# A dilated convolution with gates on one core: the first block's transposed remainder copied by VectorE alone, the last two gates in tiles of their own, the last stores dealt 5, 5, 2

## The chip, the cores and the metric

The kernel runs on one core of a Trainium2 chip. The metric is the device time of one execution in microseconds. Before the change, three runs took 313.39, 313.51 and 313.54 us; the median is 313.51 us.

The engines are named as in the profile: PE is TensorE (PEld its weight loads), ACT is ScalarE, DVE is VectorE, POOL is GpSimd and SP is SyncE, which only issues transfers here.

## What is computed

```python
B, T, D, K = (2, 16000, 144, 15)          # x: (B, T, D), w: (K, D, 2 * D), w_o: (D, D), all bf16
dil = 2
pad = (K - 1) * dil
xp = jnp.pad(x, ((0, 0), (pad, 0), (0, 0)))
h = sum(jnp.einsum('btc,cd->btd', xp[:, pad - i * dil:pad - i * dil + T, :], w[i]) for i in range(K))
z = jnp.tanh(h[..., :D]) * _sigmoid(h[..., D:])
return z @ w_o
```

It is a causal convolution of 15 taps with dilation 2 from 144 to 288 channels, a gate, and a projection back to 144 channels. (The loop over the taps is written as one sum here.)

## The kernel before

**Work.** The positions are split into eleven blocks: five pairs of full blocks (even and odd positions) and a short last one. Each block gives two units of work, the last block one, so there are 21 units, 0 to 20. A unit computes twelve columns of outputs for 128 rows. Of the 144 input channels the first 128 go through PE as they are; the other 16, the *remainder*, are gathered for eight taps at a time into one further matmul with the weights `Wr`.

**Sums.** The taps are combined with a fast convolution scheme. From the loaded tile `xn` VectorE forms, for each block, sums and differences S, D and E and from these S2, S4, S42, D2, D4, D42, E2 and E4 (line 316, as most of VectorE's work). From the weights it and PE with ScalarE form the matching tap sums `G`, `Gm`, `H`, `HH`, `GD` once at the start (lines 554 and 572; PE sums weights by matmuls with an identity). A unit has four streams, S, D, F and G. For a stream PE does the steps VV, V2a, V2b, for S and D also AV, and then A00, A01, A10, A11; ScalarE copies between the PSUM pairs in between (cVV at line 677, cV at line 683, eAV at line 695) and reads out S and D (ev, line 761); VectorE combines them into `y` (av, U, y1, y0F, y1F, y0G, y1G). Then come tanh and sigmoid (th and sg, lines 744 and 746), their product z (zm), a transposing transfer, the projection (OP0 and OP1) and its copy (os, line 882).

**Remainder of the first block.** For most blocks the transposed remainder R comes by transfers. For the first block `sums_front` makes it at lines 413 to 434: PE transposes sixteen 128x128 pieces into the two banks of a PSUM pair (trR, line 420); ScalarE copies the first bank to R and VectorE the second (cpR, line 427, 128x1024 bf16 each); PE then writes zeros over both banks (zR, line 432), which frees the pair. This is done twice, for units 0 and 1. The F and G parts of `Wr` are loaded by fifteen small transfers from GpSimd's queue (wrl, line 540); VectorE forms the S and D parts from them (wr).

**The end.** The last unit's outputs go out in twelve columns. Columns 8 to 11 (stream F) and 0 to 3 (stream G) are gated, transposed on PE (tr, line 844), copied out by VectorE (cp, line 855) and projected (OPe, line 491); columns 4 to 7 take a transfer (z4T) and one projection. ScalarE copies the results (ose, lines 830 and 852), and each column is stored by a transfer of its own (line 914). The gates of G are for columns 0 and 1 together, then 2, then 3. Each of these gates takes the only buffer of `th8` and of `sg8` with `new(0)`, so it waits for the users of the one before it. For columns 2 and 3, y1G is two sums of 128x288.

**What sets the order.** The table `ORDER` lists for each engine, for SP's transfers (DMA) and for the PSUM pairs (banks) in which order the steps are emitted; `place` goes through these lists and uses costs and latencies (the arguments of `add`) only to interleave them. Each engine and each queue works its list from front to back.

Of the kernel before, what the change touches and what calls it, by code (L numbers as in the profile page):

```python
# [26 lines left out]
def t_dve(n, psum=False):  # L27
# [7 lines left out]
   -1/wsum#10 wsum#6 wsum#12 wsum#4 wsum#16 wsum#8 wsum#2 wsum wsum#14 0/VVF V2bF V2aF VVG -1/trR 0/V2aG V2bG A01F A11F -1/zR 0/A10F A00F A00G A11Fr  # L35
   A01G A10Fr A00Fr A10G A01Fr A11G A00Gr A01Gr 1/AVS 0/VVS A11Gr A10Gr AVS V2aS V2bS -1/trR#1 0/A00S A01S A11S A00Sr A01Sr -1/zR#1 0/A10S VVD A10Sr
   A11Sr AVD V2aD V2bD 1/VVS 0/A01D A00D A01Dr A00Dr 1/V2aS V2bS 0/A11D A10D A11Dr A10Dr 1/A00S A01S A10S AVD VVD A11S V2aD V2bD VVF A10D A11D A00D
   A01D V2bF V2aF VVG 2/AVS 1/A00F A01F V2bG V2aG A10F A11F A11G 2/VVS 1/A10G A00G 2/V2bS V2aS 1/A01G 2/AVD A01S A00S VVD A10S A11S V2bD V2aD 1/OP0
   2/VVF A11D A10D A00D A01D V2aF V2bF 3/AVD 2/VVG A01F A00F A10F V2bG V2aG A11F 1/OP1 2/A00G 3/VVS 2/A01G A11G A10G 3/V2aS V2bS AVS VVD A11S A10S V2bD
   V2aD A01S A00S VVF A01D A00D A11D A10D V2bF V2aF 2/OP0 3/VVG A11F A10F 4/AVS 3/V2bG V2aG A01F A00F 2/OP1 3/A00G 4/VVS 3/A01G A10G A11G 4/V2bS V2aS  # L40
   AVD VVD A10S A11S V2aD V2bD A00S A01S VVF A01D A00D A11D A10D V2bF V2aF 5/AVD 4/VVG A11F A01F A00F A10F V2bG V2aG 3/OP1 OP0 4/A00G 5/VVS 4/A01G
   5/AVS V2bS V2aS 4/A10G A11G 5/VVD A11S A10S V2bD V2aD A00S A01S VVF A00D A01D A10D A11D V2bF V2aF 4/OP0 5/VVG A01F A00F 6/AVS 5/A10F A11F V2aG V2bG
   4/OP1 6/VVS 5/A11G A10G A00G A01G 6/V2aS V2bS AVD VVD A10S A11S V2bD V2aD A01S A00S VVF A11D A10D A01D A00D V2aF V2bF 7/AVD 6/VVG A01F A11F A00F
   A10F V2aG V2bG 5/OP1 OP0 6/A11G 7/VVS 6/A10G 7/AVS V2aS V2bS 6/A00G 7/VVD 6/A01G 7/A00S V2aD V2bD A01S A10S A11S A11D VVF A10D A01D A00D V2bF V2aF
   6/OP0 7/VVG A10F A11F 8/AVS 7/A01F A00F V2bG V2aG 6/OP1 8/VVS 7/A00G A01G 8/AVD V2aS V2bS 7/A10G 8/VVD 7/A11G 8/A01S A00S V2bD V2aD A10S A11S VVF
   A01D A00D A11D A10D V2bF V2aF 9/AVD 8/VVG A01F A11F A10F A00F V2bG V2aG 7/OP1 OP0 8/A11G A10G 9/VVS 8/A01G A00G 9/V2aS V2bS AVS VVD A11S A10S V2aD
   V2bD A00S A01S VVF A00D A01D A10D A11D V2bF V2aF 8/OP0 9/VVG A01F A11F A00F A10F 10/AVS 9/V2bG V2aG 8/OP1 10/VVS 9/A01G A00G 10/AVD V2aS V2bS 9/A10G
   10/VVD 9/A11G 10/A01S V2aD V2bD A00S A10S A11S A11D VVF A10D A01D A00D V2aF V2bF 11/AVD 10/VVG A10F A00F V2aG A11F 9/OP1 10/A01F V2bG 9/OP0 11/VVS
   10/A10G A11G A01G A00G 11/V2aS V2bS AVS VVD A11S A10S V2bD V2aD A00S A01S VVF A10D A11D V2bF V2aF A01D A00D 10/OP0 11/A10F VVG A01F 12/AVS 11/A11F
   A00F V2aG V2bG 10/OP1 12/VVS 11/A00G A01G 12/AVD V2bS V2aS 11/A11G 12/VVD 11/A10G 12/A01S V2bD V2aD A00S A10S A11S A00D VVF A01D A11D A10D V2aF V2bF  # L50
# [194 lines left out]
def kernel(  # L245
# [157 lines left out]
    def sums_front(want):  # L403
# [7 lines left out]
        for r in range(2):  # L411
# [11 lines left out]
            for h, (eng, c) in enumerate((("ACT", t_act(8 * P)), ("DVE", t_dve(8 * P)))):  # L423
                def cp(h=h, pr=pr, R=R):
                    src = banks[pr.slot][:, h, 0:512].bitcast(BF16)
                    dst = R.tile[:, 2 * h:2 * h + 2].rearrange("p s k n -> p (s k n)")
                    K_(nc.vector.tensor_copy(out=dst, in_=src) if h else nc.scalar.copy(out=dst, in_=src))  # L427
# [292 lines left out]
    def unit(ui, bi, r, base):  # L720
# [57 lines left out]
        for k, j in (("F", 2), ("G", 0)):  # L778
            op = ALU.add if k == "F" else ALU.subtract
            for b2, pair in enumerate(conv(bi, r, k, base, AT, av)):  # L780
# [7 lines left out]
                for c, n in ((0, 1), (1, 1)) if last and k == "G" and b2 else ((0, 2),):  # L788
# [3 lines left out]
                    if last and k == "G":  # L792
                        gate(c0 + c, n, t0 + .8)
# [203 lines left out]
```

## Time and profile before

| | |
|---|---|
| runs (3) | 313.39 to 313.54 us, median 313.51 |
| profiled execution | 313.12 us |
| its span, first to last instruction | 311.3 us |
| mean granted TensorE clock | 0.993 |
| busy: PE, VectorE, ScalarE, GpSimd | 297.5, 276.5, 269.0, 27.0 us |
| first matmul of unit 0 | 14.46 us |
| last projection's start | 305.29 us |
| last two stores' issue on ScalarE | from 306.18 us, 2.35 us |

Rows of the timeline give start, duration, engine, line, operation, output and inputs; in brackets stands how long the engine was idle before, and what ended that. A row with `x8` merges eight instructions. Matmul ends are modelled, so a PE gap is best read from the starts of matmuls.

### The profile page before, as it was taken

To read this page: it belongs to the slowest core of one execution; us is meant where nothing else is said; L and a number is where in the kernel's file an instruction comes from. 1 tells how busy PE (TensorE), PEld (TensorE's weight loads), DVE (VectorE), ACT (ScalarE), POOL (GpSimd) and SP (SyncE) were. 2 spreads that over 40 slices of the span, in tenths; PEclk is the share of its full clock that TensorE was granted. 3 is DMA by queue.
4 is the path that set the end of the run, shared out by engine and by line. 5 is a ranking of instruction groups with operands and counts; after the bars stand their busy time and mean duration, and the time that the engine had idled before them with its cause. 6 is when DMAs were issued, how large, how long until landed. Compare 5 with 4: busy or idle time off the path is not lost.

```text
span 311.3 us, 6703 instructions
## 1 busy us (share of the span) xinstructions
PE 297.5 (96%) x2604; PEld 276.5 (89%) x2604; DVE 276.5 (89%) x393; ACT 269.0 (86%) x449; POOL 27.0 (9%) x63
## 2 busy tenths in 40 slices
PE   8998899999999999999999999999999999999981
PEld 3797789999999999999999999999999999999881
DVE  4878999999999999899999999989996998899861
ACT  1658789998989989999998999989888999989982
POOL 9830500000000000000000000000000000000013
PEclk9999999999999999999999999999999999999997
DMA  7995569597799866986796698455886647254344
GB/s 199 107 127 118 150 67 174 140 115 153 126 162 282 215 159 104 142 199 155 189 210 98 118 181 182 138 127 162 146 187 80 123 141 231 73 128 114 59 170 131
DMA packets 153110, 45.78 MB, mean 147 GB/s; under 512 B 137061, under 2 KB 151701, under 8 KB 153078
## 3 DMA queue, kind: packets, MB, share of 16 engines
q1 hardware_dynamic: 151610, 44.59, 69.6%
q0 software_dynamic: 1216, 0.70, 1.1%
q8 instruction: 20, 0.33, 0.5%
q14 instruction: 12, 0.10, 0.1%
q10 hardware_dynamic: 252, 0.06, 0.1%
HBM read 13.31 MB, written 11.84 MB: 81 GB/s over the span
## 4 chain that ended last, share of the span: by engine, by line
PE 80%; ACT 13%; DVE 3%; issue 3%; DVEq 0%; ACTq 0%
PE acc L491 77%; ACT m L761 4%; ACT acc L683 3%; PE acc L527 2%; ACT acc L677 1%; ACT sg L746 1%; ACT th L744 1%; ACT R L427 1%; DVE D L316 1%; DVE S L316 1%; PE acc L420 1%; DVE y L316 1%; ACT os L882 0%; ACT av L695 0%; ACT osl L852 0%
## 5 line engine op out<-in xcount | busy, mean ns | idle before, releaser
L491 PEld LDWEIGHTS <-E 128*128 128x128 bf16 x882 | 112.2, 145 | 7.9 <-issue 4.0
L491 PE MATMUL acc<-w_all,E 128*128 128x288 bf16 x630 | 101.2, 286 | 1.0 <-ACT acc L683 0.3
L491 PE MATMUL acc<-Wr,R 128*128 128x288 bf16 x336 | 94.9, 286 | 0.0
L316 DVE TENSOR_TENSOR y<-U,acc 128x576 bf16<-128x576 bf16 (+1 forms) x81 | 59.4, 744 | 9.9 <-PE acc L491 6.5
L683 ACT ACTIVATE acc<-acc 128x576 f32<-128x576 f32 x84 | 54.1, 645 | 7.2 <-PE acc L491 4.9
L761 ACT ACTIVATE m<-acc 128x576 bf16<-128x576 f32 x84 | 52.8, 651 | 4.3 <-PE acc L491 2.9
L491 PEld LDWEIGHTS <-S 128*128 128x128 bf16 x378 | 48.2, 137 | 5.2 <-issue 2.4
L491 PEld LDWEIGHTS <-D 128*128 128x128 bf16 x378 | 48.8, 137 | 4.0 <-issue 1.1
L677 ACT ACTIVATE acc<-acc 128x288 f32<-128x288 f32 x84 | 33.7, 401 | 8.0 <-PE acc L491 6.4
L746 ACT ACTIVATE sg<-y 128x576 bf16<-128x576 bf16 (+3 forms) x45 | 38.9, 872 | 0.5 <-DVE y L316 0.4
L744 ACT ACTIVATE th<-y 128x576 bf16<-128x576 bf16 (+3 forms) x45 | 38.9, 871 | 0.2
L882 ACT CAST os<-acc 128x864 bf16<-128x864 f32 x40 | 34.6, 880 | 2.0 <-DVE y L316 0.9
L316 DVE TENSOR_TENSOR m<-m,av 128x1152 bf16<-128x1152 bf16 x42 | 30.5, 753 | 6.5 <-ACT m L761 6.3
L491 PE MATMUL acc<-wo_ab,zT 128*128 128x144 bf16 x480 | 35.2, 226 | 0.1
L491 PEld LDWEIGHTS <-zT 128*128 128x128 bf16 x480 | 32.2, 98 | 1.5 <-issue 0.3
L491 PEld LDWEIGHTS <-R 128*128 128x128 bf16 x336 | 32.8, 98 | 0.2
L491 PE MATMUL acc<-G,S 128*128 128x288 bf16 x147 | 30.3, 286 | 0.4 <-ACT acc L683 0.2
L491 PE MATMUL acc<-Gm,D 128*128 128x288 bf16 x147 | 29.7, 285 | 0.3
L695 ACT ACTIVATE av<-acc 128x576 bf16<-128x576 f32 x42 | 27.2, 648 | 3.0 <-PE acc L491 2.4
L491 PE MATMUL acc<-H,E 128*128 128x288 bf16 x168 | 28.1, 286 | 1.1 <-ACT acc L677 1.1
L316 DVE TENSOR_TENSOR E<-E 128x1792 bf16<-128x1792 bf16 (+1 forms) x22 | 28.1, 1286 | 0.0
L316 DVE TENSOR_TENSOR z<-th,sg 128x576 bf16<-128x576 bf16 (+3 forms) x45 | 25.5, 573 | 2.1 <-ACT sg L746 1.4
(75 smaller groups left out, 330.0 us busy)
## 6 DMA issues: line engine op xcount, KB each, us to landing
R<-q SPq DMA_DIRECT2D x19, 512.0 KB
out_dram<-os SPq DMA_DIRECT2D x8, 864.0 KB
q<-T SPq DMA_DIRECT2D x10, 256.0 KB
out_dram<-os SPq DMA_DIRECT2D x2, 519.8 KB
xt<-in_x_dram SPq DMA_DIRECT2D x6, 156.0 KB
w_all<-in_w_dram SPq DMA_DIRECT2D x3, 288.0 KB
out_dram<-os SPq DMA_DIRECT2D x2, 337.5 KB
zT<-z SPq DMA_TRANSPOSE x20
```

The source lines that it names most:

```text
L316: return K_(nc.vector.tensor_tensor(out=out_, in0=a, in1=b, op=op))
L420: K_(nc.tensor.transpose(to, ap(st.tile, c, [1, P]), ident[:, 0, :]))
L427: K_(nc.vector.tensor_copy(out=dst, in_=src) if h else nc.scalar.copy(out=dst, in_=src))
L491: K_(nc.tensor.matmul(bank, lhsT=l(), rhs=r, start=start and q == 0, stop=end and q == len(jobs) - 1, skip_group_check=True))
L527: K_(nc.tensor.matmul(banks[i % 4][:, (i // 4) % 2, :], lhsT=wz[:, 0:P], rhs=wz[:], start=True, stop=True))
L677: add("ACT", t_act(D2), lambda: K_(nc.scalar.activation(out=banks[X.slot][:, 1, 0:D2], in_=banks[X.slot][:, 0, 0:D2], func=ACT.Copy, scale ...
L683: s = add("ACT", t_act(2 * D2), lambda: K_(nc.scalar.activation(out=banks[Y.slot][:, :, 0:D2], in_=banks[X.slot][:, :, 0:D2], func=ACT.Cop ...
L695: add("ACT", t_act(2 * D2), lambda: K_(nc.scalar.activation(out=av.tile[:, SPLIT.index(k)], in_=banks[W.slot][:, :, 0:D2], func=ACT.Copy, ...
L744: add("ACT", t_act(n * D, False), lambda: K_(nc.scalar.activation(out=a_, in_=y_[0], func=ACT.Tanh)), r=[*need, y], w=[th], want=t0, name= ...
L746: add("ACT", t_act(n * D, False), lambda: K_(nc.scalar.activation(out=b_, in_=y_[1], func=ACT.Sigmoid)), r=[*need, y], w=[sg], want=t0 + . ...
L761: add("ACT", t_act(2 * D2), lambda pair=pair, i=i, b2=b2: K_(nc.scalar.activation(out=m.tile[:, i, 2 * b2:2 * b2 + 2, :], in_=banks[pair.s ...
L882: K_(nc.scalar.copy(out=dst, in_=banks[pr.slot][:, :, 0:3 * D].rearrange("p h (q d) -> p h q d", d=D)))
```

## The change

Three steps are edited, four costs that only guide the order are set anew, and the whole `ORDER` table is written in another order.

```diff
-            for h, (eng, c) in enumerate((("ACT", t_act(8 * P)), ("DVE", t_dve(8 * P)))):
-                def cp(h=h, pr=pr, R=R):
-                    src = banks[pr.slot][:, h, 0:512].bitcast(BF16)
-                    dst = R.tile[:, 2 * h:2 * h + 2].rearrange("p s k n -> p (s k n)")
-                    K_(nc.vector.tensor_copy(out=dst, in_=src) if h else nc.scalar.copy(out=dst, in_=src))
-                add(eng, c, cp, r=[pr.part[h]], w=[R], pairs=[pr], want=want + 2 + 8 * r, name="cpR")
+            def cp(pr=pr, R=R):
+                src = banks[pr.slot][:, :, 0:512].bitcast(BF16)
+                dst = R.tile[:].rearrange("p (h s) k n -> p h (s k n)", h=2)
+                K_(nc.vector.tensor_copy(out=dst, in_=src))
+
+            add("DVE", 0.07 + 16 * P / 1700, cp, r=[*pr.part], w=[R], pairs=[pr], want=want + 2 + 8 * r, name="cpR")
...
-            add("POOL", 0.55, lambda k=k, j=j0 + j, c=c: K_(nc.gpsimd.dma_start(out=Wr[c:c + CR, KI[k], :], in_=w[j, P:D, :])), w=[gWr[k]], want=-27, lat=6.0, name="wrl")
+            add("POOL", 0.55, lambda k=k, j=j0 + j, c=c: K_(nc.gpsimd.dma_start(out=Wr[c:c + CR, KI[k], :], in_=w[j, P:D, :])), w=[gWr[k]], want=-27, lat=5.0, name="wrl")
...
-            th, sg = (v[4 if n == 4 else 8].new(0) for v in (th_b, sg_b))
+            own = last and n < 4
+            th, sg = (Gen(v[8].gens[0]) if own else v[4 if n == 4 else 8].new(0) for v in (th_b, sg_b))
+            if own:
+                th.tile, sg.tile = (v[8].tiles[0][:, c0:c0 + n, :] for v in (th_b, sg_b))
...
-            need = [yg[c] for c in at[::2]]
+            need = [yg[c - c % 2] for c in at[::2]]
...
-                for c, n in ((0, 1), (1, 1)) if last and k == "G" and b2 else ((0, 2),):
-                    add("DVE", t_dve(n * D2, True), lambda pair=pair, c0=c0, b2=b2, op=op, c=c, n=n: tt(
-                        y.tile[:, c0 + c:c0 + c + n, :], U.tile[:, 2 * b2 + c:2 * b2 + c + n, :], banks[pair.slot][:, c:c + n, 0:D2], op),
-                        r=[*pair.part[c:c + n], U], w=[*gens(c0 + c, n), y], want=t0, pairs=[pair], name=f"y{b2}{k}")
-                    if last and k == "G":
+                add("DVE", t_dve(2 * D2, True), lambda pair=pair, c0=c0, b2=b2, op=op: tt(
+                    y.tile[:, c0:c0 + 2, :], U.tile[:, 2 * b2:2 * b2 + 2, :], banks[pair.slot][:, :, 0:D2], op),
+                    r=[*pair.part, U], w=[*gens(c0, 2), y], want=t0, pairs=[pair], name=f"y{b2}{k}")
+                if last and k == "G":
+                    for c, n in ((0, 1), (1, 1)) if b2 else ((0, 2),):
                         gate(c0 + c, n, t0 + .8)
...
-        store_last(c, os[c // 6], done_[c], len(units) * TU + 4 + q / 4, "POOL" if c > 5 else "ACT" if c in (1, 3) else "DMA")
+        store_last(c, os[c // 6], done_[c], len(units) * TU + 4 + q / 4, "POOL" if c in (6, 8, 9, 10, 11) else "ACT" if c in (1, 3) else "DMA")
```

So the copy of R is one instruction of 128x2048 on VectorE; the gates of columns 0 and 1, of 2 and of 3 write disjoint slices of one `th8` and one `sg8` tile and wait for each other no more; y1G is one sum of 128x576, which needs both A10G and A11G; and column 7's store goes from GpSimd to SP, which leaves five on GpSimd, five on SP and two on ScalarE. The other cost changes are those of the stores. Of the table one line of PE's shows what is written anew:

```diff
-   -1/wsum#10 wsum#6 wsum#12 wsum#4 wsum#16 wsum#8 wsum#2 wsum wsum#14 0/VVF V2bF V2aF VVG -1/trR 0/V2aG V2bG A01F A11F -1/zR 0/A10F A00F A00G A11Fr
+   -1/wsum#10 wsum#6 wsum#12 wsum#4 wsum#16 wsum#8 wsum#2 wsum wsum#14 0/VVF V2aF V2bF VVG -1/trR 0/V2aG V2bG A01F A11F A10F -1/zR 0/A00F A10Fr A01Fr
```

PE now has A10F ahead of the first zeroing (zR), and uses the F remainder weights (A10Fr) right after A00F. Ahead of the second zeroing it now has A10S, A11S and both their remainder matmuls as well. ScalarE's first cast is now of PE's first weight sum (wsum#10) and its second step the copy of one weight into H; HH for G, which needs that copy, has become VectorE's fourth weight product.

VectorE, from the long E sum of the first block (`E_88`) to the weights `wr` (`Wr<-Wr`) and the sums behind them, before:

```order
L316 TENSOR_TENSOR E_88<-E_82 128x2560
L427 COPY R_73<-acc_64 128x1024
L316 TENSOR_TENSOR S_80<-xn_67 128x2048
L554 TENSOR_TENSOR GD<-Gm,w_all 128x288
L316 TENSOR_TENSOR st_71<-xt_70 128x2x128
L316 TENSOR_TENSOR D_81<-xn_67 128x2048
L316 TENSOR_TENSOR S_84<-S_80 128x1536
L316 TENSOR_TENSOR st_71<-xt_70 128x2x128
L316 TENSOR_TENSOR D_86<-D_81 128x1536
L554 TENSOR_TENSOR Wr<-Wr 128x288
L316 TENSOR_TENSOR S_90<-S_80 128x768
```

The same place now (`S_84` is S4, `S_90` S2, `S_94` S42, `D_86` D4):

```order
L316 TENSOR_TENSOR E_88<-E_82 128x2560
L426 COPY R_73<-acc_65 128x2048
L316 TENSOR_TENSOR S_80<-xn_67 128x2048
L316 TENSOR_TENSOR S_84<-S_80 128x1536
L554 TENSOR_TENSOR Wr<-Wr 128x288 x2
L316 TENSOR_TENSOR st_71<-xt_70 128x2x128
L316 TENSOR_TENSOR S_90<-S_80 128x768
L316 TENSOR_TENSOR D_81<-xn_67 128x2048
L316 TENSOR_TENSOR S_94<-S_84 128x1280
```

The two `wr` products have moved ahead of D and D4, right behind S4, and the GD product has moved ahead of E.

GpSimd's queue, the end of the `Wr` loads; the `wo_ab` rows are loads of the projection weights. Before, the last F load is the third of the four in a row, the queue's 20th transfer, and the last G load the single one, the 23rd:

```order
L548 DMA wo_ab<-in_w_o_dram 80x144
L540 DMA Wr<-in_w_dram 16x288
L548 DMA wo_ab<-in_w_o_dram 48x144
L540 DMA Wr<-in_w_dram 16x288 x4
L547 DMA wo_ab<-in_w_o_dram 64x144
L540 DMA Wr<-in_w_dram 16x288
```

Now the last F load is the second of the last two in a row, the queue's 23rd transfer, and the last G load the single one, the 25th:

```order
L540 DMA Wr<-in_w_dram 16x288 x2
L547 DMA wo_ab<-in_w_o_dram 16x144
L548 DMA wo_ab<-in_w_o_dram 48x144
L548 DMA wo_ab<-in_w_o_dram 64x144
L540 DMA Wr<-in_w_dram 16x288 x2
L548 DMA wo_ab<-in_w_o_dram 128x144
L540 DMA Wr<-in_w_dram 16x288
```

So the last F load has moved back by three transfers and the last G load by two.

ScalarE at the end, from the last casts of the last full block (`os`) on; `osl` is the output tile of the last unit. Before:

```order
L882 CAST os_148<-acc_64 128x6x144
L852 CAST osl_150<-acc_65 128x288
L744 ACTIVATE th_139<-y_132 128x144
L746 ACTIVATE sg_141<-y_132 128x144
L852 CAST osl_150<-acc_64 128x288
L744 ACTIVATE th_139<-y_132 128x144
L746 ACTIVATE sg_141<-y_132 128x144
L830 CAST osl_150<-acc_65 128x288
L830 CAST osl_149<-acc_65 128x288
L852 CAST osl_149<-acc_66 128x144
L852 CAST osl_149<-acc_64 128x144
L852 CAST osl_149<-acc_65 128x288
```

Now:

```order
L884 CAST os_148<-acc_66 128x6x144
L747 ACTIVATE th_139<-y_132 128x288
L749 ACTIVATE sg_141<-y_132 128x144 x2
L747 ACTIVATE th_139<-y_132 128x144 x2
L854 CAST osl_150<-acc_65 128x288
L832 CAST osl_149<-acc_64 128x288
L854 CAST osl_150<-acc_63 128x288
L832 CAST osl_150<-acc_64 128x288
L854 CAST osl_149<-acc_63 128x288
L854 CAST osl_149<-acc_64 128x144
L854 CAST osl_149<-acc_65 128x144
```

All four small activations now stand in a row ahead of the casts, and the cast of columns 4 and 5 (L832, `osl_149`), which SP's first store waits for, comes before that of 6 and 7.

156 lines of the change are left out of this document (78 added, 78 removed).

## The prediction

> **What bounds the kernel now.** I read the page's busy line first, then the stages, then the two places where PE stands still: the front and the end.
>
> ```profile
> span 311.3 us, 6703 instructions
> ...
> PE 297.5 (96%) x2604; PEld 276.5 (89%) x2604; DVE 276.5 (89%) x393; ACT 269.0 (86%) x449; POOL 27.0 (9%) x63
> ```
>
> The windows view, one unit of work (13.2 us) to a row, says where the missing 4% of PE lies; its columns are the engines' busy times.
>
> ```profile
> 26.40:39.60 13.20, 10.99 (x82) 9.46 (x81) 11.74 (x17) 10.54 (x20) 4.73 (x9) 1.00 0.74 150
> 39.60:52.80 13.20, 12.75 (x107) 11.78 (x106) 12.82 (x17) 11.94 (x21) 0.00 (x0) 1.00 0.84 122
> 52.80:66.00 13.20, 13.14 (x118) 12.46 (x117) 12.81 (x20) 11.85 (x21) 0.62 (x1) 1.00 0.52 128
> ```
>
> PE is full from 52.8 us on (13.14 of 13.20), so whatever the front gains or loses is carried to the end. VectorE has 0.39 us to spare in the same row, and in 39.6 to 52.8 even less room than PE. The change acts on the front, where PE is not full, and on the end. Of the middle the new order lists move only neighbours: between each pair of sums that wait for each other stands the same PE work as before in nearly every unit, so I count 0 for it, with 0.2 either way.
>
> **The first remainder copy.** Here is the copy out of PSUM by line, and then PE around both copies.
>
> ```profile
> L427 ACT COPY R<-acc x2: 1012/1012/1012, 17.2 to 26.0; 128x1024 bf16<-128x1024 bf16 x2
> L427 DVE COPY R<-acc x2: 692/692/692, 18.3 to 27.1; 128x1024 bf16<-128x1024 bf16 x2
> ```
>
> ```profile
> 17.64 1.14 PE L491 MATMUL acc<-w_all,E 128*128 128x288 bf16 x8
> 19.03 0.41 PE L432 MATMUL acc<-wz 128*128 128x288 bf16 x2 [0.25 <-DVE R L427]
> 19.28 1.51 PE L491 MATMUL acc<-w_all,E 128*128 128x288 bf16 x11
> 20.62 0.29 PE L491 MATMUL acc<-Wr,R 128*128 128x288 bf16 x1
> ...
> 27.83 0.41 PE L432 MATMUL acc<-wz 128*128 128x288 bf16 x2 [0.77 <-DVE R L427]
> ...
> 30.86 0.53 PE L491 MATMUL acc<-Gm,D 128*128 128x288 bf16 x3
> ```
>
> And VectorE around them:
>
> ```profile
> 15.18 1.48 DVE L316 TENSOR_TENSOR E<-E 128x2560 bf16<-128x2560 bf16 x1
> 18.29 0.69 DVE L427 COPY R<-acc 128x1024 bf16<-128x1024 bf16 x1 [1.63 <-ACT R L427]
> ...
> 27.09 0.69 DVE L427 COPY R<-acc 128x1024 bf16<-128x1024 bf16 x1 [0.70 <-ACT R L427]
> 27.70 0.62 DVE L316 TENSOR_TENSOR D<-D 128x768 bf16<-128x768 bf16 x1
> 28.23 1.75 DVE L316 TENSOR_TENSOR E<-xn 128x3072 bf16<-128x3072 bf16 x1
> 30.76 1.23 DVE L316 TENSOR_TENSOR S<-xn 128x2048 bf16<-128x2048 bf16 x1 [0.77 <-PE acc L491]
> ```
>
> The two halves do not run side by side: VectorE's starts 0.04 us after ScalarE's ends, both times. So a pair costs 1.01 + 0.69 = 1.70 us, and ScalarE is freed of 2.02 us in all. What does 128x2048 on VectorE alone cost? The small copies out of PSUM at the end give the slope:
>
> ```profile
> L855 DVE COPY zt<-acc x5: 280/410/421, 300.2 to 304.8; 72x512 bf16<-72x512 bf16 x3, 72x256 bf16<-72x256 bf16 x2
> ```
>
> 0.28 us for 256, 0.42 for 512 and 0.69 for 1024 elements are a fixed 0.14 and 0.54 per 1024, so 1.23 to 1.38 (twice 0.69); I take 1.25. That is 0.45 less than the pair. "PSUM — Partial Sum Buffer", section Specifications (TRN2), in the Trainium skill says that ScalarE and VectorE read PSUM in parallel at full rate if they use different banks; by that the split pair would end after 1.01 us and the change would cost 0.24 a copy. The rows of line 427 show no overlap, so the sum goes by them.
>
> Early in its list VectorE now forms a difference of G weights (HH, as its fourth weight product; before, it came after E2) that needs ScalarE's copy of one weight:
>
> ```profile
> 8.90 0.64 ACT L572 CAST GD<-acc 128x576 bf16<-128x576 f32 x1 [6.67 <-PE acc L491]
> ...
> 12.87 0.43 ACT L612 COPY H<-w_all 128x288 bf16<-128x288 bf16 x1
> ```
>
> ScalarE's first cast now belongs to PE's first sum, 8 matmuls of 0.122 us (the spacing in 17.64's row of eight matmuls) earlier than 8.90, at 7.92; 0.64 and 0.43 later, at 8.95 or so, that product can start. With what stands between it and the long E sum, that sum ends at about 17.65 instead of 16.66. PE reaches the matmuls that read it at 17.64, so that costs 0 to 0.3; I take 0. The copy then runs from 17.7 to 18.95. PE has twelve matmuls (1.47 us) ahead of the zeroing at line 432 instead of eight (0.98), and gets there at 19.15: the gap before 19.03 is gone (0.41 from start to start; the row's 0.25 counts from a matmul's modelled end), and PE stands 0.37 us ahead.
>
> **What is late next** are the remainder weights Wr, loaded by GpSimd's queue:
>
> ```profile
> L540 POOL DMA_DIRECT2D Wr<-in_w_dram x15: 484/490/662, 3.1 to 17.6; - x15
> ...
> DMA to landing us min/median/max: 2.8/3.8/4.6
> ```
>
> The last of these loads starts at 17.55 (17.6 in the row), as the queue's 23rd DMA. In the new order the last F load is the 23rd and the last G load the 25th, so they start at about 17.55 and 18.6 and land at 21.35 (20.35 to 22.15) and 22.4 (21.4 to 23.2). PE wants the F weights after A00F, at 19.9 (before: at 20.62, with no wait), so a wait of 1.45 us (0.45 to 2.25) comes in place of the 0.41. VectorE's `wr` pair waits for the G loads: S and S4 stand ahead of it, which end at about 21.0, so W = 1.4 us (0.4 to 2.2), and everything behind it on VectorE waits too.
>
> **The second copy.** VectorE, from the end of the first copy to the long E sum of the next block: before 18.98 to 28.23 = 9.25. Now less 0.70 (the wait for ScalarE), less 0.22 (a GD product already formed), plus 0.56 (the longer copy) plus W: 8.9 + 1.4 = 10.3, so E starts at 29.3 (28.3 to 30.1), and the copy, which stands 1.3 us ahead of it, ends at 28.0. PE: F-load wait included, its second transposes end near 26.7, then twelve matmuls instead of eight, to 28.2, so the zeroing is at 28.2 instead of 27.83. Behind it PE no longer has 0.49 us of S matmuls, and ScalarE has already read out both S pairs, so the D matmuls at 30.86 follow 2.4 instead of 3.03 us after the zeroing: 30.6. PE is 0.25 ahead. VectorE's S sum starts at 31.0 rather than 30.76; the wait of 0.77 for PE covers the rest. ScalarE now does its 0.57 us sigmoid of unit 0 before the tanh that waits for VectorE's y, so its chain to the end of unit 1 gains what VectorE's 0.25 takes, and 0.3 more.
>
> Front: **0.3 us gained**. At the early ends of the landings 1.0 gained; at the late ends PE's D matmuls come at 31.4 and the front loses 0.5.
>
> **The end.** VectorE, ScalarE and the stores:
>
> ```profile
> 301.45 0.82 DVE L316 TENSOR_TENSOR y<-U,acc 128x288 bf16<-128x288 bf16 x2 [0.45 <-PE acc L491]
> ...
> 303.99 0.23 DVE L316 TENSOR_TENSOR z<-th,sg 128x144 bf16<-128x144 bf16 x1 [1.18 <-ACT sg L746]
> ```
>
> ```profile
> 303.85 0.69 ACT L830 CAST osl<-acc 128x288 bf16<-128x288 f32 x2
> 304.81 0.28 ACT L852 CAST osl<-acc 128x144 bf16<-128x144 f32 x1 [0.27 <-PE acc L491]
> 305.88 0.58 ACT L852 CAST osl<-acc 128x144 bf16<-128x144 f32 x2 [0.79 <-PE acc L491]
> 306.18 2.35 ACTq L914 DMA_DIRECT2D out_dram<-osl  x2
> ```
>
> ```profile
> L914 POOL DMA_DIRECT2D out_dram<-osl x6: 614/616/666, 302.4 to 305.6; - x6
> L914 SPq DMA_DIRECT2D out_dram<-osl x4: 786/844/877, 304.6 to 307.3; - x4
> ```
>
> Before, the last two gates share a tile with each other and with the one ahead, and ScalarE does an output cast between them: z of the last column comes 2.5 us after the y's start. With slices of their own all four activations run in a row (about 1.0 us), and the last z comes near 304.1 in spite of y, which is one 128x576 sum of 0.75 us now and is formed 0.1 earlier. PE meets as much waiting in the last unit as before by my count (1.9 against 1.7 us up to the last projection), but its own last products move from 305.29 to about 304.9, and ScalarE's last casts end 0.4 earlier. ScalarE's two stores start 0.43 earlier, at 305.75. SP: its first store waits for the first half of line 830's pair, which now comes first, so it starts near 304.05 instead of 304.6; five at 0.844 end at 308.25, where four ended at 307.3 + 0.84 = 308.1. So SP takes over from ScalarE, whose last issue ended at 308.53. The end moves by **0.3 us**, with 0.45 if ScalarE's pair still decides, and 0.1 the other way if SP's fifth lands as late after its issue as its fourth did before.
>
> **Sum**: 0.3 + 0.3 = 0.6 off the profiled execution of 313.12 us (span 311.3 and 1.8 around it), 312.5; the median of the runs, 313.51, lies 0.39 above that execution, so 312.9 in those terms.
>
> **Rivals.**
> 1. *The wait for Wr takes the place of the wait for ScalarE* (ends slower). Place: VectorE's `wr` sums and PE's first Wr matmul. If the last G load lands at 23.2, E starts at 30.1, 1.9 late, of which 0.77 is covered: VectorE brings 1.1 into units 1 and 2, where it has 0.4 us a unit to spare. Less the 0.3 of the end that is 0.7 to 0.8: 314.2. It decides from a landing of about 22.9 on. For it: the full VectorE rows. Against: the median of 3.8.
> 2. *The front gains nothing*, since ScalarE's chain in units 0 and 1 sets PE's pace, and the end gives 0.1 only: 313.4. For it, from the waits of PE (us in total, times, longest), a group as long as any other:
>
> ```profile
> PE acc L491 <- ACT acc L677: 1.3, 3, 0.6
> ```
>
> 3. *Both gains in full*, 1.0 and 0.45: 312.1. Needs the loads at their earliest.
> 4. *The two halves were worth having in parallel*: each copy then ends 1.25 - 1.01 = 0.24 later than it could, 0.5 in all, less the 0.3 of the end: 313.7. This is what would follow from the Trainium skill's rule on PSUM, told above. The starts of the halves, one behind the other, speak against it.
>
> **How the numbers follow.** Chances: forecast 0.38, rivals 0.27, 0.18, 0.14 and 0.03. The time is the forecast's 312.9; its own range is 312.5 to 313.2. For 8 in 10 the range runs from just under rival 3's time to rival 1's, 312.0 to 314.2. A difference under 0.2% (0.63 us) is about what a measurement of this kernel cannot tell from none; the forecast lies at that bound. Faster: 0.24 of the forecast and 0.14. Same: 0.14, 0.17 of rival 2, 0.05 of rival 1 and 0.03. Slower: the rest of rival 1 and 0.01 of rival 2.
>
> **What would show it.** One copy row of 128x2048 near 1.25 us, without a wait for ScalarE; no PE gap ahead of the first zeroing; a PE wait ahead of the first Wr matmul, and VectorE idle before `wr` (this is the step I trust least: without it the gain grows to 1). At the end ScalarE's four small activations in a row, and SP's fifth store as the last to be issued. Wrong would be a VectorE copy over 1.4 us, gaps in units 1 and 2 that VectorE ends, or new gaps in PE's middle.

## The result: slower, with the loss in the front and behind the last projection

The changed kernel takes 316.11 us (four runs, 315.89 to 316.27) where the kernel before takes 313.45 (four runs, 313.37 to 313.54): a ratio of 1.0079, 95% interval 1.0053 to 1.0106. I had forecast 312.9 with a range up to 314.2, so the prediction is wrong in sign and range.

The page's busy line of the changed kernel says where it is not: PE's work is the same (297.6 us, 2604 matmuls), and the span has grown by 2.9 us.

```profile
span 314.2 us, 6711 instructions
...
PE 297.6 (95%) x2604; PEld 276.3 (88%) x2604; DVE 276.7 (88%) x392; ACT 267.0 (85%) x447; POOL 26.3 (8%) x62
```

**The front.** PE in the timeline of the changed kernel: its first V.V product (the origin of the marks below), the first zeroing, the first matmuls with Wr, the second zeroing and the first D matmuls.

```profile
14.31 0.41 PE L491 MATMUL acc<-HH,E 128*128 128x288 bf16 x2
...
18.96 0.41 PE L432 MATMUL acc<-wz 128*128 128x288 bf16 x2
19.21 0.65 PE L491 MATMUL acc<-w_all,E 128*128 128x288 bf16 x4
21.60 0.65 PE L491 MATMUL acc<-Wr,R 128*128 128x288 bf16 x4 [1.74 <-DMA wo_ab<-in_w_o_dram]
...
28.73 0.41 PE L432 MATMUL acc<-wz 128*128 128x288 bf16 x2
...
31.52 0.28 PE L491 MATMUL acc<-Gm,D 128*128 128x288 bf16 x1 [0.34 <-ACT acc L683]
```

VectorE there:

```profile
15.36 1.49 DVE L316 TENSOR_TENSOR E<-E 128x2560 bf16<-128x2560 bf16 x1
17.16 1.22 DVE L426 COPY R<-acc 128x2048 bf16<-128x2048 bf16 x1 [0.31 <-PE acc L420]
...
21.99 0.53 DVE L554 TENSOR_TENSOR Wr<-Wr 128x288 bf16<-128x288 bf16 x2 [1.48 <-DMA wo_ab<-in_w_o_dram]
...
27.20 1.23 DVE L426 COPY R<-acc 128x2048 bf16<-128x2048 bf16 x1 [0.64 <-ACT acc L683]
```

The copy is one row of 1.22 us without a wait for a copy of ScalarE's (the 0.64 of the second row is for another step), and the gap ahead of the first zeroing is gone. In its place stands a PE wait of 1.74 us for a transfer. The profile names a `wo_ab` load as the one that came last, a neighbour on GpSimd's queue; the matmul reads Wr, and GpSimd's own rows show that the last F load of Wr (the second of the pair at 16.67, so from about 17.16) and the last G load (18.24) are that late:

```profile
16.67 0.98 POOL L540 DMA_DIRECT2D Wr<-in_w_dram  x2
...
18.24 0.49 POOL L540 DMA_DIRECT2D Wr<-in_w_dram  x1
```

**The end.** First ScalarE, then SP in the changed kernel:

```profile
301.67 1.65 ACT L884 CAST os<-acc 128x864 bf16<-128x864 f32 x2
...
303.55 0.54 ACT L749 ACTIVATE sg<-y 128x144 bf16<-128x144 bf16 x2
303.97 0.53 ACT L747 ACTIVATE th<-y 128x144 bf16<-128x144 bf16 x2
...
307.03 2.57 ACTq L916 DMA_DIRECT2D out_dram<-osl  x2
```

```profile
303.34 0.83 SPq L908 DMA_DIRECT2D out_dram<-os  x2
305.48 5.20 SPq L916 DMA_DIRECT2D out_dram<-osl  x5
```

The four small activations run in a row, as planned. But the casts (`os`) of the last two block outputs end at 303.32, and SP issues their stores, the last two big ones, at 303.34 and 303.7; before, they went at 300.0 and 301.5:

```profile
L906 SPq DMA_DIRECT2D out_dram<-os x2: 350/350/350, 300.0 to 301.5; - x2
...
DMA to landing us min/median/max: 2.1/2.7/3.7
```

The last row is for GpSimd's stores of single output columns (column stores below). Here are the column stores of the changed kernel, again with the landing of GpSimd's, then the windows view of its end (after the busy times of the engines come the granted PE clock, the busy share of the DMA engines and GB/s):

```profile
L916 POOL DMA_DIRECT2D out_dram<-osl x5: 614/617/661, 305.1 to 307.6; - x5
L916 SPq DMA_DIRECT2D out_dram<-osl x5: 775/882/1445, 305.5 to 309.9; - x5
L908 SPq DMA_DIRECT2D out_dram<-os x2: 356/390/425, 303.3 to 303.7; - x2
...
DMA to landing us min/median/max: 4.3/4.7/4.8
```

```profile
305.00:307.00 2.00, 1.10 (x13) 0.60 (x10) 0.72 (x3) 1.58 (x6) 1.91 (x4) 1.00 1.05 429
307.00:309.00 2.00, 0.00 (x0) 0.00 (x0) 0.00 (x0) 0.19 (x2) 1.19 (x2) 1.00 0.92 308
309.00:311.00 2.00, 0.00 (x0) 0.00 (x0) 0.00 (x0) 0.00 (x0) 0.00 (x0) 0.75 0.70 149
```

While GpSimd issues its column stores (from 305.1) the DMA engines are full with block data (1.05, 429 GB/s), and these stores land a median of 4.7 us after their issue; before, it was 2.7. The engines were just as full before (1.10 and 432 GB/s from 303 to 305), but there the block data had ended 0.09 us before the last two projection matmuls began.

**Marks.** To compare profiles I count from PE's first V.V product (the 14.31 above), since the first loads ahead of it take between 13.70 and 14.57 us in profiles, in kernels that are alike up to there too. A is the start of unit 2's V.V product of F, B that of unit 20's V.V product of G, C the start of the last two projection matmuls (306.39 - 14.31 = 292.08 in the changed kernel), "tail" the span's end less C (314.2 - 306.39 = 7.81), each read from PE's rows in the trace.

| kernel | ratio to before (95%) | A | B | C | tail |
|---|---|---|---|---|---|
| before | 1 | 35.97 | 277.55 | 291.09 | 5.75 |
| after | 1.0079 (1.0053 to 1.0106) | 36.76 | 279.30 | 292.08 | 7.81 |
| e1, the edits in the old order | 0.9987 (0.9978 to 0.9996) | 35.35 | 276.91 | 290.38 | 5.76 |
| e2, the new order, old edits | 1.0095 (1.0081 to 1.0110) | 36.86 | 279.05 | 292.30 | 7.20 |
| e3, after with Wr loads early | 1.0044 (1.0031 to 1.0056) | 35.44 | 277.63 | 290.40 | 7.88 |
| e4, after with the old tail | 1.0064 (1.0050 to 1.0078) | 36.72 | 279.21 | 293.26 | 5.77 |
| e5, after, block stores of one row | 1.0035 (1.0021 to 1.0049) | 36.79 | 279.30 | 292.08 | 5.93 |
| e6, copy only | 0.9980 (0.9972 to 0.9989) | 35.34 | 276.91 | 290.45 | 5.88 |
| e7, deal only | 0.9995 (0.9986 to 1.0004) | 35.97 | 277.52 | 291.06 | 5.81 |
| e8, gates only | 0.9998 (0.9989 to 1.0007) | 35.99 | 277.55 | 291.02 | 5.83 |
| e9, e1 with deal 7, 4, 1 | 0.9970 (0.9954 to 0.9986) | 35.35 | 277.05 | 290.52 | 5.51 |
| e10, e1 with deal 6, 5, 1 | 0.9986 (0.9967 to 1.0004) | 35.35 | 276.91 | 290.38 | 6.19 |
| e11, e9 with the gates in a row | 0.9964 (0.9946 to 0.9983) | 35.80 | 277.36 | 290.38 | 5.91 |
| e12, e1 with block stores late | 1.0094 (1.0075 to 1.0114) | 36.21 | 278.04 | 291.51 | 8.71 |

After against before, from the first V.V product to the end: 0.99 at C and 2.06 in the tail, 3.05 us together. That is the difference of these two profiles; the medians of the runs differ by 2.66. One profile stands behind each row of marks, several runs behind each ratio. How well a mark repeats can be seen at A: 35.34 or 35.35 in the four profiles with the new copy and no Wr wait (e1, e6, e9, e10), 35.97 to 35.99 with the old copy (before, e7, e8), and 36.72 to 36.86 in the four with the late Wr loads (after, e2, e4, e5).

### The profile page after: what moved, and what is told of

Same layout as the page of the kernel before. It is cut to its first block, busy times and chain, and to the rows that moved or that the text cites. A ratio compares the mean times of both kernels' runs of the same rounds, so it can differ in the third digit from the quotient of the medians.

```text
span 314.2 us, 6711 instructions
## 1 busy us (share of the span) xinstructions
PE 297.6 (95%) x2604; PEld 276.3 (88%) x2604; DVE 276.7 (88%) x392; ACT 267.0 (85%) x447; POOL 26.3 (8%) x62
## 4 chain that ended last, share of the span: by engine, by line
PE 75%; ACT 12%; POOL 5%; DMA 2%; issue 2%; DVE 2%; POOLq 0%; ACTq 0%; DVEq 0%
PE acc L491 75%; ACT m L764 4%; ACT acc L683 3%; DMA wo_ab<-in_w_o_dram 2%; POOL Wr L540 2%; ACT acc L677 1%; ACT os L884 1%; DVE y L316 1%; POOL out_dram L916 1%; POOL wo_ab L548 1%; ACT th L747 1%; ACT sg L749 1%; POOL wo_ab L544 1%; ACT av L695 1%; DVE m L316 0%
## 5 line engine op out<-in xcount | busy, mean ns | idle before, releaser
L316 DVE TENSOR_TENSOR y<-U,acc 128x576 bf16<-128x576 bf16 x80 | 59.1, 752 | 9.5 <-PE acc L491 6.9
```

The lines of the kernel that those rows point to most:

```text
L316: return K_(nc.vector.tensor_tensor(out=out_, in0=a, in1=b, op=op))
```

## The experiments

My theory after the result was that the edits are harmless and the rewritten order costs at two places (ORDER); the rival was that the edits themselves cost, by a longer copy and a fifth store on SP (EDITS).

### e1: the three edits in the old order

```diff
 ACT:
-   ... 0/cVVG -1/cpR 0/cVG ... 0/cVS -1/cpR#2 0/ev0S ...
+   ... 0/cVVG 0/cVG ... 0/cVS 0/ev0S ...
 DVE:
-   ... E4 cpR#1 S ... wr#1 cpR#3 D2 ... 20/y1G y1G#1 cp ...
+   ... E4 cpR S ... wr#1 cpR#1 D2 ... 20/y1G cp ...
 DMA:
-   20/store store#1 store#9 store#12 store#8 store#10
+   20/store store#1 store#9 store#7 store#12 store#8 store#10
 POOL:
-   20/store#4 store#5 store#2 store#3 store#6 store#7
+   20/store#4 store#5 store#2 store#3 store#6
```

> The three edits of the change (the copy of both banks by VectorE, the two last gates in tiles of their own with the one y product, the deal 5, 5, 2) in the old order of steps, where only the steps that the edits remove or move differ. Theory ORDER (the loss is in the order that was rewritten with the change, at the Wr loads and at the block stores): the time is within 0.6 us of the kernel before, PE has no wait for a DMA before its first Wr matmul, and the block stores of the last unit are issued near 300. Theory EDITS (the edits themselves cost: a longer copy in the front, a fifth store on SP at the end): 1.5 to 2.7 us slower than the kernel before, with the loss behind the last projection.

312.52 us, ratio 0.9987: the change as it is described makes the kernel faster, by 0.1%. (The four new costs that guide the order are in this kernel too.) PE has no wait for a DMA ahead of its first Wr matmul, and the block stores go at 299.3 and 300.7:

```profile
L916 POOL DMA_DIRECT2D out_dram<-osl x5: 614/617/666, 301.7 to 304.2; - x5
L916 SPq DMA_DIRECT2D out_dram<-osl x5: 768/828/872, 303.8 to 307.4; - x5
L908 SPq DMA_DIRECT2D out_dram<-os x2: 351/351/351, 299.3 to 300.7; - x2
...
DMA to landing us min/median/max: 2.4/3.0/3.7
```

EDITS falls.

### e2: the new order with the old edits

```diff
 ACT:
-   ... 20/th0 sg2 sg3 th2 th3 ose#2 ...
+   ... 20/th0 sg2 th2 sg3 th3 ose#2 ...      (and cpR, cpR#2 where they were)
 DVE:
-   ... 20/y1G cp ...
+   ... 20/y1G y1G#1 cp ...
 POOL:
-   20/store#3 store#2 store#4 store#6 store#5
+   20/store#3 store#2 store#4 store#6 store#5 store#7
```

> The other way round: the new order of steps with the old code (copy split between ScalarE and VectorE, y product in two halves, gates in shared tiles, deal 6, 4, 2); two small activations of the last gates are exchanged, since the shared tiles do not allow the new sequence. ORDER: 2.0 to 3.0 us slower than the kernel before, with the same wait of 1.5 to 2 us at the first Wr matmul and block stores issued after 303. EDITS: less than 1.0 us slower.

315.95 us, ratio 1.0095: the order alone costs as much as the whole change. The wait at the first Wr matmul is 1.49 us, and the block stores go at 302.8 and 303.2, about the 303 that I had said. Together e1 and e2 settle that the loss belongs to the order. In e2, as in the changed kernel, A is late (36.86 against 36.76) although e2 has the old copy: the copy's gain of 0.63 at A (e6 below) is seen in the old order only, and in the new one the wait for Wr takes nearly all of it. The landing of GpSimd's column stores (2.5 to 3.6 us, median 2.9) is no longer than in e1, since less of the block data is left when they are issued; the tail is 7.20 all the same.

### e3: the changed kernel with the Wr loads in their old places

```diff
 POOL:
-   -1/wrl#11 wrl#6 wrl#2 wrl#12 wz wrl wo72 wol#3 wol#8 wol#11 wrl#14 wrl#8 wol#2 wrl#7 wrl#9 wrl#5 wol#1 wrl#4 wrl#3 wol#14 wol#5 wol#7 wrl#10 wrl#1
-   wol#15 wrl#13 wol#10 wol#13 wol wol#4 wol#12 wol#9 wol#6 4/tz 6/tz ...
+   -1/wrl#10 wrl#9 wrl#5 wrl#1 wrl wz wol#14 wrl#4 wol#10 wo72 wol#2 wrl#13 wol#13 wrl#7 wrl#6 wol#9 wrl#11 wol#5 wrl#12 wrl#3 wrl#2 wrl#14 wol#8 wrl#8
+   wol#11 wol#1 wol#4 wol#7 wol#3 wol#6 wol#12 wol wol#15 4/tz 6/tz ...
```

> The changed kernel with GpSimd's loads of the front in the old order, so that the last Wr load of F is the 21st instead of the 24th DMA and the last of G the 24th instead of the 26th. If the late loads cost the front its 0.66 us: the wait of 1.74 at the first Wr matmul goes or falls under 0.5, PE passes its later marks 0.6 to 0.9 us earlier than in the changed kernel, and the time is 315.2 to 315.6 us if the end does not give it back. Rival (the front is late for another reason, VectorE's longer copy or the changed order of E and the remainder): the wait moves to another releaser and the time stays at 315.9 to 316.3.

314.29 us, ratio 1.0044 instead of 1.0079. PE's wait has almost gone; it goes from the E matmuls of A00F to its Wr matmuls 0.78 us after they began, of which 0.29 is a gap, against 2.39 after:

```profile
19.41 0.65 PE L490 MATMUL acc<-w_all,E 128*128 128x288 bf16 x4
20.19 0.66 PE L490 MATMUL acc<-Wr,R 128*128 128x288 bf16 x4
```

The gain is 1.32 us at A and 1.68 at C, more than the 0.6 to 0.9 that I expected: I had compared after with before, where the copy's gain had hidden part of the loss. VectorE still waits 1.10 us for the G loads (1.48 after), at 21.81, and that can have cost no more than the 0.09 by which e3 stands behind e1 at A. By the times the gain is smaller than by the marks: 0.35%, about 1.1 us, with intervals that touch (1.0053 to 1.0106 and 1.0031 to 1.0056); the time, 314.29, is below the 315.2 to 315.6 expected. What shows the effect is A, where e3 stands with e1 and apart from the four kernels with late loads. (The expectation counts one instruction of GpSimd's ahead of the loads that is no transfer, so its 21st and 24th, 24th and 26th are the 20th and 23rd, 23rd and 25th above.)

### e4: the changed kernel with the old tail

```diff
 PE:
-   ... 20/VVG A11F 19/OP1 20/V2aG V2bG A01F A10F A00F A01G A11G A00G 19/OP0 20/OP0 OP1 tr#1 A10G OPe#2 ...
+   ... 20/VVG 19/OP1 20/A01F A11F A10F V2bG V2aG A00F 19/OP0 20/A00G A01G OP0 OP1 tr#1 A10G A11G OPe#2 ...
 ACT:
-   ... 20/th8 sg8 19/os0 20/sg0 os0 os1 th0 sg2 sg3 th2 th3 ose#2 ose ose#3 ose#1 ...
+   ... 19/os0 20/th8 sg8 os0 sg0 th0 os1 ose#3 th2 sg2 ose#2 th3 sg3 ose#1 ose ...
 DMA:
-   20/z4T store#1 store store#9 store#7 store#10 store#12 store#8
+   20/z4T store store#1 store#9 store#7 store#12 store#8 store#10
```

(The same is done to the last steps of VectorE, the banks and GpSimd's column stores.)

> The changed kernel with the old order of the last steps on every engine (from the V.V product of the last unit on: projections, casts, block stores, and GpSimd's column stores), deal 5, 5, 2 kept. If the block stores issued 3.3 us later cost the end by filling the DMA engines when the column stores come: they are issued near 301 again, the last column store lands 2 to 2.8 us after the last projection instead of 4.8, and the time is 313.9 to 314.6 us. Rival DEAL (the fifth store on SP, or the four on GpSimd, set the end): the stores still end near 314 and the time stays within 0.5 us of 316.1.

315.03 us, ratio 1.0064, where 313.9 to 314.6 was expected; its interval overlaps that of the changed kernel, so the time alone decides nothing. Half of it is as expected: the second block store goes 4.0 us ahead of C again (at 303.5), and the tail is 5.77 us. The other half isn't: from B to C PE takes 14.05 us with the old tail here and 12.78 with the new one, and 1.27 of the 2.04 us go again. The new tail is the better one for PE and the worse one for the stores. Why the old list takes 0.5 us longer from B to C here than in its own kernel (13.54) was not followed.

### e5: the changed kernel, block stores of one row

```diff
+                if mb == NMB - 1 and n > 48:
+                    n, dst = 1, bass.AP(out.tensor, out[b, t0 + a, 0].offset, [[48 * D, 1], [1, (e - a) * D]])
                 src = os.tile[row:row + n, 0:e - a, :].rearrange("p c d -> p (c d)")
```

> The changed kernel with the two block stores of the last unit cut from 128 rows of 6912 bytes to one row each; this leaves out 254 of the 256 row pieces that they store, and nothing else: the same instructions at the same places. COLLISION (their data, sent from 304 to 309, shares the DMA engines with the column stores): the column stores land 2.3 to 3.2 us after their issue instead of 4.3 to 4.8, the span ends 5.5 to 6.2 us after the start of the last projection instead of 7.8, and the time is 1.6 to 2.3 us under the changed kernel's 316.11. DEAL (the number of column stores on each queue sets the end): no more than 0.5 us faster.

313.90 us, ratio 1.0035. With the same instructions at the same places and A, B and C within 0.03 us of the changed kernel's, the tail falls from 7.81 to 5.93 us, and every column store of GpSimd lands after 2.0 or 2.1 us. Its column stores and its windows:

```profile
L917 POOL DMA_DIRECT2D out_dram<-osl x5: 614/617/661, 304.5 to 307.0; - x5
...
DMA to landing us min/median/max: 2.0/2.0/2.1
```

```profile
305.00:307.00 2.00, 0.98 (x10) 0.61 (x10) 0.32 (x2) 1.21 (x5) 2.00 (x5) 1.00 0.24 54
307.00:309.00 2.00, 0.00 (x0) 0.00 (x0) 0.00 (x0) 0.00 (x0) 0.58 (x1) 0.99 0.39 88
```

COLLISION holds, with 1.88 us; DEAL falls. By the ratios it is 0.44% or 1.4 us, a little under my bound of 1.6.

### e6, e7, e8: each edit alone in the old order

e6 is the kernel before with only the loop over the two halves of the copy replaced by the one `tensor_copy` of the change; e7 with only this:

```diff
-        store_last(c, os[c // 6], done_[c], len(units) * TU + 4 + q / 4, "POOL" if c > 5 else "ACT" if c in (1, 3) else "DMA")
+        store_last(c, os[c // 6], done_[c], len(units) * TU + 4 + q / 4, "POOL" if c in (6, 8, 9, 10, 11) else "ACT" if c in (1, 3) else "DMA")
```

and e8 with only `own` in `gate` and the y product in one piece. The steps of the order are those of e1, each for its own edit.

> The kernel before with the one copy of both banks by VectorE and nothing else. If the old order with all three edits owes its gain to the copy: ratio to the kernel before 0.997 to 0.9995, PE 0.5 to 0.7 us ahead at the V.V product of F of the third unit, and the same end. If VectorE's longer copy only trades one wait for another: 1.000, PE level with the kernel before there.

> The kernel before with one column store moved from GpSimd to SP (deal 5, 5, 2) and nothing else. My prediction's step gives up to 0.3 us less; by the end of the run with all edits in the old order, which is 5.8 us behind the start of the last projection as in the kernel before, it gives nothing: ratio 0.9995 to 1.0005. If SP's fifth store ends last: up to 0.4 us more.

> The kernel before with the last two gates in tiles of their own and the last y product in one piece, everything else as it was, in the old order. In the old order ScalarE still comes to the two gates one after the other, so the tiles alone give nothing: ratio 0.9995 to 1.0005, with the last z product within 0.2 us of where it was against the last projection. If the shared tiles had held the second gate: the last projection comes 0.2 to 0.4 us earlier against the first transposition of the end.

The copy alone gives 0.9980 (312.32 us); PE is 0.41 us ahead at the first zeroing (18.73 against its first V.V product at 14.57; before 19.03 against 14.46) and 0.63 at A, which stays to the end. Here is e6's copy on VectorE and PE's zeroing:

```profile
17.42 1.22 DVE L425 COPY R<-acc 128x2048 bf16<-128x2048 bf16 x1 [0.30 <-PE acc L419]
```

```profile
18.73 0.41 PE L431 MATMUL acc<-wz 128*128 128x288 bf16 x2
```

The deal (0.9995) and the gates (0.9998) give nothing that can be told from none: C is 0.03 and 0.07 us earlier, the tail 0.06 and 0.08 longer.

### e9, e10, e11: can the end be shortened in the old order?

```diff
-        ... "POOL" if c in (6, 8, 9, 10, 11) else "ACT" if c in (1, 3) else "DMA")
+        ... "POOL" if c > 5 or c == 3 else "ACT" if c == 1 else "DMA")                       # e9, e11
+        ... "POOL" if c in (3, 6, 8, 9, 10, 11) else "ACT" if c == 1 else "DMA")             # e10
 ACT:
-   20/ose#3 th2 sg2 ose#2 th3 sg3 ose#1 ...
+   20/ose#3 th2 sg2 th3 sg3 ose#2 ose#1 ...                                                # e11
```

> The three edits in the old order, with the column stores dealt 7 to GpSimd, 4 to SP, 1 to ScalarE. In the old order the span ended 5.75 to 5.88 us behind the start of the last projection with GpSimd, SP and ScalarE at 6, 4, 2 and at 5, 5, 2 alike, and ScalarE's second issue took 1.43 where its first took 0.83. SCALARE LAST: without its second store ScalarE ends at 306.2, SP at 307.4, GpSimd at about 306.6, and the span ends 0.6 to 1.0 us earlier against the last projection: ratio to the kernel before 0.9955 to 0.9975. GPSIMD'S LANDING or a fixed tail decides: no more than 0.2 us, ratio 0.998 to 0.999.

> The same with 6 to GpSimd, 5 to SP, 1 to ScalarE. If the issue that ends last sets the end, SP's fifth (to about 308.2) takes over from ScalarE's second (308.3): 0 to 0.2 us against the deal 5, 5, 2 in the old order, ratio 0.998 to 0.999. If ScalarE's second store costs by itself (its landing, not its issue): as 7, 4, 1.

> As the deal 7, 4, 1, with the four activations of the two small gates one behind the other (tanh, sigmoid, tanh, sigmoid, and then the cast that stood between them), which only tiles of their own allow. ROW: the last z product comes 0.5 to 0.6 us earlier against the V.V product of G, the last projection 0.2 to 0.3 us earlier, and the time is 0.2 to 0.3 us less than with the deal alone. CAST: the cast that comes 0.15 us later holds the banks of the next transpositions and the last projection does not move.

e9 takes 312.30 us (0.9970), e10 312.81 (0.9986), e11 312.21 (0.9964). The last two gates in a row do what ROW says on PE (z rows of VectorE in e11):

```profile
302.07 0.23 DVE L315 TENSOR_TENSOR z<-th,sg 128x144 bf16<-128x144 bf16 x1 [0.27 <-ACT sg L748]
302.50 0.23 DVE L315 TENSOR_TENSOR z<-th,sg 128x144 bf16<-128x144 bf16 x1 [0.19 <-ACT sg L748]
```

In e1 the second z came at 303.18 with B at the same 291.27 us: it is 0.68 earlier, and from B to C PE takes 13.02 instead of 13.47. But the tail is 5.91 instead of e9's 5.51, so 0.05 us is left. SCALARE LAST came for the landing and failed for the tail: with one store less on ScalarE the last store of e9 lands 0.88 us earlier after C than e1's (3.84 against 4.72), but from there to the span's end it takes 1.69 us instead of 1.03, so the tail is 0.25 shorter and not 0.6 to 1.0. Why that got longer was not followed. ScalarE's one store took 1.56 us to issue. In e10 the last landing is where it was in e1 (4.70), with SP's fifth store as the last, and the tail is longer, 6.19. Each of these tails is that of one profile. The intervals of e1, e6, e9, e10 and e11 overlap, so which of them is best stays open; all but e10 lie below the kernel before with their whole interval, and all below the changed one.

### e12: e1 with the block stores late

```diff
 DMA:
-   20/z4T store store#1 store#9 store#7 store#12 store#8 store#10
+   20/z4T store#9 store store#1 store#7 store#12 store#8 store#10
```

> The three edits in the old order, with one move on SP: the two block stores go behind SP's first column store, so that they are issued near 304.6 and 305.0 instead of 299.3 and 300.7; nothing moves on another engine, and PE ends where it did. COLLISION: the column stores of GpSimd that are issued before stay at 2 to 3 us, the later ones on all queues land 4 us or more after their issue, the span ends 7.5 us or more behind the start of the last projection instead of 5.76, and the kernel is 1.5 to 3 us slower than with the block stores early (ratio to the kernel before 1.004 to 1.009). QUEUE: only the 0.8 us that the two issues take on SP ahead of the other four column stores counts, with the landing as before: 0.2 to 0.6 us, ratio 0.9995 to 1.001.

315.81 us, ratio 1.0094. Two rows moved on SP make the good order as slow as the changed kernel. The windows of its end, and its column stores:

```profile
307.00:309.00 2.00, 0.00 (x0) 0.00 (x0) 0.00 (x0) 0.00 (x0) 0.00 (x0) 0.82 1.04 418
309.00:311.00 2.00, 0.00 (x0) 0.00 (x0) 0.00 (x0) 0.00 (x0) 0.00 (x0) 0.50 0.95 338
```

```profile
L916 POOL DMA_DIRECT2D out_dram<-osl x5: 614/614/666, 302.4 to 305.0; - x5
L916 SPq DMA_DIRECT2D out_dram<-osl x5: 822/878/1422, 304.5 to 310.3; - x5
L908 SPq DMA_DIRECT2D out_dram<-os x2: 421/443/465, 305.4 to 305.9; - x2
...
DMA to landing us min/median/max: 2.0/2.0/2.1
```

The tail is 8.71 us, 2.95 longer than e1's. GpSimd's five stores, issued ahead of the block data, land in 2.0 us; those of SP, issued behind, decide the end. So QUEUE falls as the whole cause, though part of the 2.95 is what it says: about 0.9 us is the time of the two issues themselves, which now stand ahead of four column stores on SP, and SP's five column stores take 5.63 us to issue instead of 4.42. The rest is later landing. The move is also larger than in the changed kernel: the two block stores go 0.1 us before and 0.4 after C. (This profile also has a Wr wait of 0.83 us in the front, worth 0.86 at A, as e11's has one of 0.37; that is not the move's doing. If other executions have it too, it helps the time past my 1.009.)

**When the block data ends.** The traces also hold each row that the DMA engines moved, and these rows tie the runs together. All times are us after C:

| profile | the two block stores issued | block data ends | last store lands | from there to the span's end |
|---|---|---|---|---|
| before | -5.5, -4.1 | -0.1 | 4.25 | 1.54 |
| e1 | -5.5, -4.0 | 0.0 | 4.72 | 1.03 |
| after | -3.1, -2.7 | 2.7 | 6.76 | 1.05 |
| e2 | -3.5, -3.1 | 1.85 | 5.37 | 1.87 |
| e5 | -3.1, -2.7 (one row each) | none to speak of | 4.93 | 1.00 |
| e12 | -0.1, 0.4 | 5.9 | 7.47 | 1.24 |

The two block stores go out as 256 rows of 6912 bytes, which take 4.6 to 5.0 us. A row of a column store issued behind them starts, on whichever of the three queues, only after the last block row has started, 0.18 to 0.25 us later in before, after, e1, e2, e3, e4 and e12. In the changed kernel GpSimd issues its first column store at 305.09, the last block row starts at 308.48, and the first row of that store at 308.68. So how late a column store lands goes by how much block data is still to flow when it is issued. Against before, the last landing moves by 2.51 us and the time from it to the span's end (the close) is 0.49 shorter, together the tail's 2.06 but for rounding; against e1, with the same deal of the stores, the landing makes up 2.04 and the close 0.02. Taking the data away (e5) takes 1.83 of the landing back. The close is 1.00 to 1.09 us in e1, e3, e4, e5, e7 and after, all with the deal 5, 5, 2, and 1.24 in e12; with the other deals it is 1.44 to 1.87. Why it differs was not followed.

## Why the prediction was wrong

The sum of the runs, in marks: the copy -0.64 (e6 at C), the other edits -0.07 (e1 against e6), the late Wr loads +1.68 (after against e3 at C), the rest of the order +0.02 at C (e3 against e1), the tail +2.06. Together 3.05, the difference of the two profiles (that of the medians is 2.66). Each part is read from single profiles, and the copy's share holds for the old order.

- **The copy.** Right: 1.22 us for my 1.25, no wait for a copy of ScalarE's, the 0.41 ahead of the first zeroing gone. Alone it is worth 0.64 us. The sum kept only part of that, since it set the late Wr loads against it. Rival 4 is out, since the copy alone gains. But I was wrong to let the rows speak against the rule on PSUM, "PSUM — Partial Sum Buffer", section Specifications (TRN2), in the Trainium skill: VectorE's half started late because it waited for ScalarE's to be done (its row says so), so no run here shows what two copies side by side would take.
- **The Wr wait at PE.** Right as a mechanism, and in its range: a wait of 1.90 us from start to start for a forecast of 1.45 (0.45 to 2.25). The last F load began at about 17.16, 0.4 earlier than I had put it, but PE's matmul came 4.4 us behind it where I had taken 3.8. The long E sum, which I had ending at 17.65, ended at 16.85, so this cost nothing.
- **The front's sum, 0.3 us gained.** This step failed. I let the wait be repaid behind the second copy: the zeroing at 28.2 and the D matmuls 2.4 us later. They came at 28.73 and 2.79 later, at 31.52. At A the front has lost 0.79, not gained 0.3. Of what I named, 0.45 lay in the wait itself; the rest is repayment that did not come. By e3 the late loads cost 1.32 us at A. Rival 1 is nearest: its price for the front (1.1 us into units 1 and 2) is about what e3 takes back, though through PE's own wait and not through VectorE's, which is still 1.10 us long in e3.
- **The middle, 0 within 0.2.** Too low. After less before grows from 0.79 at A to 1.75 at B. Part of it follows the Wr loads (their price grows from 1.32 to 1.67 from A to B), and with them early the new order still loses 0.09 at A and 0.72 at B (e3 against e1). It gets this back by its shorter tail on PE (12.77 from B to C in e3, 13.47 in e1). Which steps of the middle cost it was not tested.
- **The end, 0.3 us gained.** This step failed most. It counted issues: SP's five stores from 304.05 to 308.25, ScalarE's from 305.75. They ran from 305.48 to 310.68 and from 307.03. PE's part came: from B to C it takes 12.78 us for 13.54 before. Against C the column stores of SP and ScalarE start where they did (-0.91 for -0.98 and 0.64 for 0.63), so their later times in the span come with the late C. The last z came at 305.43 instead of 304.1, since y itself was formed at 302.73 and the second z stands behind two copies on VectorE. And it took the landing after an issue as given. The sum had no term for the two block stores, whose casts and issues the new order moves behind the last A matmuls: the second one went 4.05 us ahead of C before and 2.7 after, the first 5.5 and 3.1. So the block data ended 2.7 us behind C and not with it, and the last landing moved by 2.51 us. Taking the data away at these places gives 1.88 us back (e5); moving the two issues alone, and further, costs 2.95, of which some 0.9 is the issues' own time (e12).
- **The deal.** I had SP take over from ScalarE as the last to issue. That happened (310.68 against ScalarE's 309.60), and in the old order too (308.18 against 307.73 in e1). But it is worth nothing: in e7 the last store lands 0.45 us later after C than before (4.70 for 4.25), the close behind it is 0.45 shorter, and the tails are 5.81 and 5.75, so this term is 0.
- **The gates.** The activations run in a row as forecast. Alone that gives nothing in the old list (e8), and moved into a row 0.45 us on PE of which the stores give 0.4 back (e11).
- **Rivals 2 and 3.** Both are out: the copy's 0.63 at A stays to the end in e6, so ScalarE's chain does not hold the front's pace, and the loads came late and not at their earliest.

A rule of the Trainium skill would have pointed to the missing term. "DMA: Bandwidth & Descriptors", section Issuing engines are not separate DMA queues, says that transfers from SP, ScalarE and GpSimd all run on the same 16 DMA engines and interleave. The trace agrees that they share: GpSimd's stores take 2.0 us beside no block data (e5) and 4.7 with it. It shows no taking of turns with the block rows already issued: the first row of these stores starts at 308.68, 0.2 us after the last block row (308.48).

## What to carry to other kernels

When an order is rewritten, list for each queue the big transfers that have moved against the small ones at the end, and ask when their data ends against the last projection, not only when they are issued. Here two stores of 864 KB went 1.4 and 2.5 us later against it than before; that brought the last landing 2.5 us later, and the three edits had gained 0.7 at C (e1). A kernel's described edits and its re-planned order are two changes; the edits in the old order are the first experiment to make. And loads that arrive just in time (Wr) have to be kept early on their queue, since most of a wait at PE was not made good later: of 1.90 us here, 1.3 was left at A and 1.7 at C (e3). The old order stands near that edge itself, as the waits of 0.37 and 0.83 us in the profiles of e11 and e12 show.

## What the hardware showed that I had not expected

- A wait's named releaser can be a neighbour on the same queue: the changed kernel's profile gives `wo_ab`, those of e2 and e4, with the same queue, give Wr for the same wait (1.49 and 1.69 us).
- Under a full load of the DMA engines the issue gets slower too, not only the landing: SP's five column stores took 5.20 us to issue in the changed kernel (up to 1445 ns for one) and 4.42 in e1 (up to 872). With the same instructions at the same places and no block data they took 4.51 (up to 885, e5); in e12 they took 5.63.
- ScalarE's last column store takes 1.43 to 1.71 us to issue where the first of two takes 0.83 to 0.87, and a single one takes 1.43 to 1.60 (e9 to e11), so it isn't its being the second.
